# Linear attention with a feed-forward layer on one core: another order of all pieces, half of W1 centred by its column means, and five 4-byte copies among the loads

## The chip, the cores and the metric

The kernel runs on one core of a Trainium2 chip. The number that counts is the device time of one execution in microseconds (us). Of a few runs the median is taken. The core has five engines with queues of their own, each working strictly in order: TensorE (PE, matrix products), VectorE (DVE), ScalarE (ACT), GpSimd (POOL) and SyncE (SP, which here issues all transfers).

## The reference, cut to what matters

Inputs are x (4 x 8 x 768 x 32), decays a, and B and C (4 x 8 x 768 x 16). For each batch and head a state of 16 x 32 is carried along the sequence, and the attention result becomes the input of a feed-forward layer whose normalisation is folded into its first weight.

```python
M = (C_i . B_j) * exp(cum_i - cum_j) * (j <= i)      # inside a chunk
y = M @ x + (C @ state) * exp(cum)                   # plus what entered
state = decay * state + sum_j decay_from_j * B_j x_j
xn = (y - mean(y)) / sqrt(var(y) + 1e-6) * g         # y as tokens x 256
out = y + max(xn @ w1, 0) @ w2                       # w1 256 x 1024, w2 1024 x 256, 64-bit floats
```

## The kernel before, in words

The sequence is cut into 6 steps t of 128 positions; a step holds 4 x 128 = 512 tokens. Every step goes through the attention (scores `G`, weighted scores `R`, what entered `Vi`, values `V`, carried state `Z`, `K`, `S`, its block form `sb`), its output is copied out of PSUM (`y`), split into an upper and a lower float32r part (`yh`, `yl`), turned into token order (`T`, `tc`) and its mean and variance taken (`st`, `ag`, `rs`, `rc`). Then come 8 hidden products `h t m` (line 489, six matrix products of 512 columns each; weight chunk c = m // 4), each followed by `hh` (the relu, upper part) and `hl` (lower part, line 500), which frees the PSUM tile. The second product is `o t b` (line 507, 24 matrix products of 256 columns) or, for step 0, `oc` (line 517, a quarter of the hidden rows at a time); `oe` (line 522) adds the residual and `od` (line 525) stores.

The 64-bit weights are turned into float32 on the chip, half a row block of 128 x 512 at a time: `k0` absolute value of the top word (ACT, line 188), `k1` clamp (DVE, line 193), `k2` shift (DVE, 202), `k3` sign (DVE, 207), `kr` the rest from the low word (ACT, 213), `f` their sum (line 218). W1 is scaled by g and has its column mean taken off: `wc c k` (line 230) does both with two products in float32, against a matrix made from the identity and g (`gm`, lines 220 to 225) and against -g/256; `wh` and `wl` (lines 235, 239) split the result. `wc` is run four times, for (c, k) = (0,0), (0,1), (1,0), (1,1).

PSUM has two pools: 5 buffers `ps_att` for the attention and `oc`, 3 buffers `ps_ffn` for `wc`, `h` and `o`. Results `o` wait for their store in 3 SBUF buffers (pool `p3`), hidden parts in 9 each (pool `hp`).

There is no planner at run time: the order of everything is the text `ISSUE`, a list of pieces. Each piece is put on its engine's queue in that order; a suffix `:v`, `:p`, `:a` chooses VectorE, GpSimd or ScalarE instead of the piece's usual engine. `fill i n` is a product of zeros with n columns that only keeps PE busy. `ld` pieces are loads on SP, `ro` and `ld ud` take the decays of steps 2 to 5 out to memory and back.

Of the kernel before the start of the list is needed to follow the order:

```
ld c 0, l2, ini, ld sel, lr 0, e 0, ld b 0, dc 0, x 0, ld id, ones, rcl, ld w1 0 0, ru, e 1, ld w1 0 1, du 0 0, riv, fill 8 512, rd, ld bt 0, lr 1,
cx 0 0, ld x 0, du 0 1, cx 0 1, ld w1 1 1, x 1, so, ld c 1, B:v 0, dc 1, ld x 1, sm, W:v 0, ld w1 1 0, ld b 1, G 0, du 1 1, ld w2 0, mb, gm:p,
...
k3 1 1 1, ld bt 2, wh 1 0 0, ld c 2, f:v 1 1 0, tc 0 1, ld w2 3, yh:a 0 0, st 0 3, f 1 1 1, ld b 4, G 1, wh 1 0 1, ag 0 3, st 0 1, ld b 2, yh:a 0 1,
ld c 4, be:v 1, Z 0 1, W 1, ld ud 2, wc 1 0, yl 0 1, S 0 1, ld x 2, wl:v 1 0 0, ld ud 4, wl:v 1 0 1, yl 0 0, k0 2 0, R 1 1, h 0 0, ld bt 3, k0 2 2,
R 1 3, be 2, wh 1 1 0, R 1 0, kr 2 0, Z 1, R 1 2, sb 1 0, ld bt 4, hh 0 0, wl:v 1 1 0, K:p 1 0, h 0 1, W 2, k1 2 0, S 1 0, k2 2 0, wc 1 1, c2 1,
```

Of the kernel before, what the change touches and what calls it, by code (L numbers as in the profile page):

```python
# [635 lines left out]
```

## Time and profile before

| | us |
|---|---|
| median of 3 runs | 198.72 (198.05 to 199.54) |
| the profiled execution, whole | 199.18 |
| its span, first to last instruction | 197.4 |
| PE busy, share of the span | 96% |
| DVE busy, share of the span | 65% |
| ACT busy, share of the span | 35% |
| POOL busy, share of the span | 18% |

The rows shown further down come from the profiled execution. Times in them are counted from the start of the span; the 1.78 us between the span and the whole lie around it. A row of the timeline names the engine, the line, what is written and read, and in brackets how long the engine was idle before and what ended that. Products in float32 show as two records each. "PE busy" counts the fills as well.

### The profile page before, as it was taken

Reading aid. Unit: us, or ns where it says so; the run is one execution under the profiler, and the core shown is the slowest. Engines: PE = TensorE matmul, PEld = TensorE weight load, DVE = VectorE, ACT = ScalarE, POOL = GpSimd, SP = SyncE. Lnnn points to the kernel's source line nnn. Section 1 sums busy time; section 2 is a strip of 40 time slices with the busy share of each in tenths; the row PEclk is TensorE's granted clock in tenths of the full one; section 3 lists DMA queues with packets and bytes.
Section 4 is the critical chain, followed back from the end, with each engine's and each line's share of the span. In section 5 each row is a group of like instructions: output and inputs, shape, how many; then the busy total and the mean of one; then the engine's idle time right before and its main releaser. Section 6 shows DMA issues by size and latency. Waiting matters only on the chain.

```text
span 197.4 us, 6404 instructions
## 1 busy us (share of the span) xinstructions
PE 188.8 (96%) x2854; PEld 162.5 (82%) x2854; DVE 129.1 (65%) x273; ACT 69.3 (35%) x127; POOL 35.7 (18%) x41
## 2 busy tenths in 40 slices
PE   8997997999999997999999999999999999999992
PEld 8765564877898985998878998789998899988992
DVE  1789998979997847666489913847347581336610
ACT  4648996588263722000152032403002051124000
POOL 0271191654600000310630000405000000000000
PEclk9999999999999999999999999999999999999999
DMA  5999999640050014711000051000021000200002
GB/s 118 286 367 401 375 307 235 202 149 15 3 163 0 0 53 119 220 67 58 3 3 0 3 150 67 3 3 0 11 72 53 0 3 3 80 27 3 19 17 71
DMA packets 11660, 18.42 MB, mean 93 GB/s; under 512 B 2385, under 2 KB 5873, under 8 KB 11633
## 3 DMA queue, kind: packets, MB, share of 16 engines
q1 hardware_dynamic: 11632, 18.02, 28.7%
q8 instruction: 22, 0.36, 0.8%
q14 instruction: 6, 0.04, 0.1%
HBM read 14.74 MB, written 3.28 MB: 91 GB/s over the span
## 4 chain that ended last, share of the span: by engine, by line
PE 90%; DVE 3%; ACT 3%; DMA 2%; issue 1%; POOL 0%; DVEq 0%
PE ph L489 32%; PE po L507 29%; PE pp L517 5%; PE yps L402 4%; PE wc L230 4%; PE G L375 4%; PE idle L534 4%; PE yps L394 3%; PE yt L458 3%; PE Z L414 2%; DMA out_dram<-o 2%; DVE hl L500 1%; DVE o L522 1%; ACT y L441 1%; PE cum L271 1%
## 5 line engine op out<-in xcount | busy, mean ns | idle before, releaser
L507 PE MATMUL po<-w,hh 128*128 128x256 f32 x320 | 56.8, 281 | 0.1
L489 PE MATMUL ph<-yh,w 128*128 128x512 f32 x192 | 53.8, 402 | 0.5 <-DVE hl L500 0.5
L507 PEld LDWEIGHTS po<-w,hh 128*128 128x128 f32 x320 | 49.1, 188 | 1.0 <-DVE hl L500 0.4
L507 PE MATMUL po<-w,hl 128*128 128x256 f32 x160 | 44.7, 279 | 0.0
L494 ACT ACTIVATE hh<-ph 128x512 fp32r<-128x512 f32 x34 | 20.2, 598 | 68.7 <-PE ph L489 59.8
L489 PEld LDWEIGHTS ph<-yh,w 128*128 128x128 f32 x192 | 34.3, 188 | 7.9 <-DVE hl L500 0.8
L500 DVE SCALAR_TENSOR_TENSOR hl<-ph,hh 128x512 fp32r<-128x512 f32 x48 | 32.3, 683 | 11.4 <-ACT hh L494 11.2
L507 PEld LDWEIGHTS po<-w,hl 128*128 128x128 f32 x160 | 30.1, 188 | 0.0
L489 PE MATMUL ph<-yl,w 128*128 128x512 f32 x96 | 29.8, 392 | 0.0
L522 DVE SCALAR_TENSOR_TENSOR o<-po,rstd,ytok 128x256 f32<-128x256 f32 x20 | 9.5, 480 | 27.3 <-PE po L507 27.2
L489 PEld LDWEIGHTS ph<-yl,w 128*128 128x128 f32 x96 | 18.0, 188 | 4.2 <-DVE yl L450 0.3
L381 DVE TENSOR_TENSOR R<-G,WW 128x512 f32<-128x512 f32 x24 | 15.7, 677 | 2.4 <-PE G L375 2.4
L450 POOL TENSOR_TENSOR yl<-y,yh 128x512 fp32r<-128x512 f32 x6 | 8.4, 1403 | 35.2 <-DVE yh L447 22.0
L496 DVE TENSOR_SCALAR hh<-ph 128x512 fp32r<-128x512 f32 x14 | 9.5, 681 | 4.9 <-PE ph L489 4.9
L441 ACT COPY y<-yps 128x256 f32<-128x256 f32 x15 | 5.2, 374 | 18.8 <-PE yps L402 15.1
L517 PE MATMUL pp<-w,hh 128*128 128x256 f32 x64 | 11.4, 281 | 0.0
L470 DVE BATCH_NORM_STATS2 st<-ytok 128x6 f32<-128x256 f32 x24 | 9.9, 416 | 1.4 <-ACT ytok L463 1.4
L517 PEld LDWEIGHTS pp<-w,hh 128*128 128x128 f32 x64 | 9.9, 188 | 0.3
L361 ACT COPY WW<-wt 32x1024 f32<-32x1024 f32 x8 | 8.3, 1040 | 5.1 <-DVE R L381 5.0
L534 PE MATMUL idle<-const-float32-0.0 128*128 128x128 f32 (+3 forms) x34 | 9.2, 425 | 0.8 <-PEq L624 0.8
L402 PE MATMUL yps<-R,xt 64*32 64x64 f32 x768 | 9.2, 226 | 0.0
L345 POOL TENSOR_TENSOR bs<-b,ud 128x512 f32<-128x512 f32 x3 | 3.9, 1293 | 28.6 <-DMA b<-in_bn_dram 28.6
(96 smaller groups left out, 229.7 us busy)
## 6 DMA issues: line engine op xcount, KB each, us to landing
raw<-in_w_dram SPq DMA_DIRECT2D x8, 512.0 KB, 9.0
xt<-in_x_dram SPq DMA_DIRECT2D x6, 512.0 KB, 6.0
out_dram<-o SPq DMA_DIRECT2D x24, 128.0 KB, 1.7
ud<-scr SPq DMA_DIRECT2D x8, 256.0 KB
c<-in_cn_dram SPq DMA_DIRECT2D x6, 256.0 KB, 2.8
b<-in_bn_dram SPq DMA_DIRECT2D x6, 256.0 KB, 7.2
bt<-in_bt_dram SPq DMA_DIRECT2D x6, 256.0 KB, 8.9
cf<-in_sums_dram SPq DMA_DIRECT2D x1, 256.0 KB
```

The source lines that it names most:

```text
L381: nc.vector.tensor_tensor(out=R.rearrange("p b i k -> p b (i k)"), in0=tiles.pop(("G", t, q)).rearrange("p b i k -> p b (i k)"), in1=WW.re ...
L402: nc.tensor.matmul(tiles["y", t, g, f][32 * k:32 * k + 32, b], x[r, b * NH + h], tiles["R", t, h // 2][r, b, h % 2], start=(t + f + b == 0 ...
L450: e.tensor_tensor(out=tiles["yl", t][:, g], in0=tiles["y32", t][:, g], in1=tiles["yh", t][:, g].bitcast(F32), op=ALU.subtract)
L470: nc.vector.bn_stats(out=st, in_=tiles["ytok", t][:, b])
L489: nc.tensor.matmul(ph, W1[m // 4, k][:, s, mc], v[:, k], start=(i == 0), stop=(i == len(cmb) - 1))
L494: e.activation(h, tiles["ph", t, m], AF.Relu)
L496: e.tensor_scalar(out=h, in0=tiles["ph", t, m], scalar1=0.0, scalar2=None, op0=ALU.max)
L500: nc.vector.scalar_tensor_tensor(out=l, in0=tiles.pop(("ph", t, m)), scalar=0.0, in1=tiles["hh", t, m].bitcast(F32), op0=ALU.max, op1=ALU. ...
L507: nc.tensor.matmul(po, tiles[v, t, m][:, cols], W2[m // 2,][:, s, (m % 2) * DM:(m % 2 + 1) * DM], start=(n == 0), stop=(n == len(cmb) - 1))
L517: nc.tensor.matmul(tiles["po", t, b], tiles[v, t, m][:, cols], W2[m // 2,][:, s, (m % 2) * DM:(m % 2 + 1) * DM], start=(c + n + b % 2 == 0 ...
L522: nc.vector.scalar_tensor_tensor(out=o, in0=tiles.pop(("po", t, b)), scalar=tiles["rstd", t][:, b], in1=tiles["ytok", t][:, b], op0=ALU.mu ...
L534: nc.tensor.matmul(ps[:, :n], zero.to_broadcast([P, P]), zero.to_broadcast([P, n]), start=True, stop=True)
```

## The change

Every piece keeps its arithmetic except the centring of chunk 0 of W1 and the engine that some pieces run on. The parts are:

1. For chunk c = 0 of W1, `wc 0 0` and `wc 0 1` (two products each) are replaced by one `wm 0` (two products with -g/256 that give the column mean times g for both row blocks) and two VectorE instructions `wf 0 k`, each of which scales its 128 x 512 block by g and adds the mean out of PSUM. Chunk 1 keeps `wc`, and it is now loaded, converted and used first (`h 0 4` is the first hidden product).
2. `gm` runs on ScalarE and no longer computes +g/256 apart.
3. The whole list is written anew: other positions, other engines for some pieces, and 9 fills instead of 17. To name the larger shifts between engines, VectorE gets four more of `cm`, two more each of `hh`, `y`, `yh`, and the two `wf`, and loses two each of `K`, `c2`, `f`, `wl`; GpSimd gets two more each of `K`, `c2`, `f`, `wl` and loses `gm`, one `W` and three `sb`; ScalarE gets four `sb`.
4. Five pieces `pc` on SP copy 4 bytes of a tile that a load filled into a tile that nobody reads. Each waits until that load has landed, and the loads behind it in the list wait with it.
5. Results get a pool of 6 buffers (before: 3), hidden parts 10 each (before: 9), `R` 9 (before: 8).

```diff
-    rp = pool("rp", 8)
-    hp = pool("hp", 9)
+    rp = pool("rp", 9)
+    hp = pool("hp", 10)
+    op = pool("op", 6)
...
+    def after(i, what, *at):
+        src = W1[at].bitcast(F32) if what == "w1" else W2[at].bitcast(F32) if what == "w2" else tiles[(what, *at)]
+        src = src.rearrange("p r d -> p (r d)") if what == "x" else src
+        nc.sync.dma_start(seen[:, 8 * i:8 * i + 1], src[:1, :1])
...
     def centring(e=nc.vector):
-        e.tensor_scalar(out=gm, in0=gt, scalar1=1.0 / DM, scalar2=None, op0=ALU.mult)
-        e.tensor_scalar(out=gneg, in0=gt, scalar1=-1.0 / DM, scalar2=None, op0=ALU.mult)
-        for k in range(KC):
-            e.tensor_scalar(out=gd[:, k], in0=ident, scalar1=gt[:, k:k + 1], scalar2=gm[:, k:k + 1], op0=ALU.mult, op1=ALU.subtract)
+        if e is nc.scalar:
+            e.activation(gneg, gt, AF.Copy, scale=-1.0 / DM)
+            for k in range(KC):
+                e.activation(gd[:, k], ident, AF.Identity, bias=gneg[:, k:k + 1], scale=gt[:, k:k + 1])
...
+    def mean_of(c):
+        w = centre[c] = ps_ffn.tile([P, 512], F32, tag="ffn", name=f"wm{c}")
+        for k in range(KC):
+            nc.tensor.matmul(w, gneg[:, k:k + 1].to_broadcast([P, P]), f32[1, c, k], start=(k == 0), stop=(k == KC - 1))
+
+    def less_mean(c, k):
+        f = f32[1, c, k]
+        nc.vector.scalar_tensor_tensor(out=f, in0=f, scalar=gt[:, k:k + 1], in1=centre[c], op0=ALU.mult, op1=ALU.add)
...
     def diagonal(t, f, e=nc.gpsimd):
-        e.tensor_tensor(out=sb, in0=tiles[("S", *before(t, f))], in1=blkt.unsqueeze(1).to_broadcast([P, NB, 2 * HD]), op=ALU.mult)
+        S = tiles[("S", *before(t, f))]
+        if e is nc.scalar:
+            for i in range(2):
+                e.activation(sb[:, :, i * HD:(i + 1) * HD], S[:, :, i * HD:(i + 1) * HD], AF.Copy, scale=even[:, i:i + 1])
...
     def finished(t, b):
-        o = tiles["o", t, b] = p3.tile([P, DM], F32, tag="o", name=f"o{t}{b}")
+        o = tiles["o", t, b] = op.tile([P, DM], F32, tag="o", name=f"o{t}{b}")
...
+fill 0 512, ld la, ld sums, ld mask, ld c 0, fill 1 512, ld w1 1 1, l1, ini, l2, lr 0, dc 0, ld id, ones:v, ld b 0, e 1, ld sel, du 0 0, fill 2 128,
+ld w1 1 0, fill 3 64, x 1, fill 4 256, cx 0 1, ld bt 0, so, ld x 0, cx 0 0, k0 1 1 1, fill 5 256, ld as, fill 6 256, sm, lr 1, k1 1 1 1, e 0, W:v 0,
+du 0 1, fill 7 256, kr 1 1 1, dc 1, mb, x 0, az, B:v 0, k0 1 1 0, k2 1 1 1, G 0, C:v 0, kr 1 1 0, be:v 0, du 1 1, fill 8 128, sp, k1 1 1 0, k3 1 1 1,
+em 0, ld bt 1, ld g, ld w1 0 0, ld w1 0 1, ld c 1, ld w2 0, Z 0 0, em 1, c2:p 0, R 0 0, S 0 0, R 0 1, sb:a 0 1, Z 0 1, f 1 1 1, R 0 3, gm:a, Vi 0,
+R 0 2, V 0 0, k0 1 0 0, k2 1 1 0, V 0 1, k3 1 1 0, y 0 0 0, pc 0 w1 0 1, kr 1 0 1, f:v 1 1 0, wc 1 1, ld x 1, y 0 1 1, rcl, k0 1 0 1, ld w2 3, inv,
+k1 1 0 0, pc 7 bt 0, ru, y 0 0 1, kr 1 0 0, k2 1 0 0, ld w2 1, wc 1 0, k1 1 0 1, ld b 1, be:v 1, ld c 2, k3 1 0 0, ro 0, k2 1 0 1, ld b 2, f:v 1 0 0,
+pc 2 w1 0 0, k3 1 0 1, ld bt 2, riv, f:v 1 0 1, rd, ro 1, ld x 2, wh 1 1 1, y 0 1 0, du 1 0, yh:a 0 1, T 0 1, C 1, wh 1 1 0, Z 1, yh:a 0 0, T 0 0,
+yl 0 1, tc 0 1, wm 0, tc 0 0, W 1, wl:v 1 1 0, yl 0 0, wl:v 1 1 1, h 0 4, ld bt 3, wf 0 0, K:p 0 1, st 0 3, B 1, wf 0 1, h 0 5, hh 0 4, S 0 1,
+wh 1 0 1, ld ud 2, K 1 0, wh:v 1 0 0, cm 1 0, h 0 6, S 1 0, cm 1 1, wl:v 1 0 0, sb 1 1, kr 2 3, hl 0 4, G 1, hh 0 6, wl 1 0 1, ag 0 3, st 0 0,
+hh 0 5, hl 0 6, k0 2 1, h 0 2, R 1 0, c2:p 1, kr 2 0, R 1 2, k0 2 0, sb 1 0, h 0 1, R 1 3, hh 0 2, K:p 1 1, R 1 1, C 2, hl 0 2, W 2, Vi 1, hl 0 5,
...
+st 5 1, h 5 6, ag 5 1, hl 5 7, hh 5 3, hl 5 3, h 5 0, ag 5 0, rs 5, hh 5 6, rc 5, hl 5 6, h 5 5, hh 5 0, hl 5 0, hh 5 5, hl 5 5, o 5 0, o 5 2,
+oe 5 0, od 5 0, od 4 2, od 1 0, od 4 3, o 5 1, o 5 3, oe 5 1, oe 5 2, od 5 1, od 0 2, od 3 0, od 5 2, oe 5 3, od 5 3
```

## Rows read from the trace of the kernel before

**Rows 1.** The page: busy time of each engine over the span.

```profile
PE 188.8 (96%) x2854; PEld 162.5 (82%) x2854; DVE 129.1 (65%) x273; ACT 69.3 (35%) x127; POOL 35.7 (18%) x41
```

**Rows 2.** Busy time by 10 us: PE, PEld, DVE, ACT, POOL, PE clock, DMA share, GB/s.

```profile
0.00:10.00 10.00, 8.75 (x81) 7.81 (x85) 4.86 (x12) 5.78 (x11) 1.45 (x8) 1.00 0.71 201
10.00:20.00 10.00, 8.66 (x268) 5.98 (x251) 9.45 (x17) 6.39 (x16) 4.41 (x6) 1.00 1.02 387
20.00:30.00 10.00, 9.75 (x147) 5.63 (x147) 9.77 (x20) 9.86 (x18) 6.12 (x6) 1.00 1.06 337
...
50.00:60.00 10.00, 10.00 (x249) 9.29 (x248) 9.86 (x23) 4.43 (x9) 2.54 (x3) 1.00 0.26 82
...
70.00:80.00 10.00, 8.77 (x168) 6.98 (x168) 6.92 (x17) 1.60 (x3) 0.00 (x0) 1.00 0.39 122
```

**Rows 3.** The chain of waits in order of time: start, duration, what.

```profile
20.82 3.44 PE wc L230 x8
24.26 1.24 PE G L375 x59
...
41.64 0.79 PE Z L414 x53
...
108.15 11.20 PE po L507 x96
...
193.76 0.48 DVE o L522
```

**Rows 4.** Timeline, PE and VectorE: from `be` of step 0 to the first hidden product.

```profile
12.80 1.25 DVE L354 TENSOR_TENSOR be<-bt,pend 128x512 f32<-128x512 f32 x1
...
26.49 1.28 DVE L239 TENSOR_TENSOR w<-wc,w 128x512 fp32r<-128x512 f32 x2
...
27.43 1.49 PE L489 MATMUL ph<-yh,w 128*128 128x512 f32 x4
```

**Rows 5.** Groups by line: count, busy us, mean ns of one, idle before.

```profile
L381 DVE TENSOR_TENSOR R<-G,WW 128x512 f32<-128x512 f32 x24 | 15.7, 677 | 2.4 <-PE G L375 2.4
...
L450 POOL TENSOR_TENSOR yl<-y,yh 128x512 fp32r<-128x512 f32 x6 | 8.4, 1403 | 35.2 <-DVE yh L447 22.0 <-ACT yh L447 13.1
...
L207 DVE SCALAR_TENSOR_TENSOR top<-raw,top 128x512 int32<-128x512 int32 x8 | 5.3, 687 | 0.1
...
L326 POOL TENSOR_TENSOR cs<-c,ud 128x512 f32<-128x512 f32 x3 | 3.8, 1272 | 2.9 <-issue 2.9
...
L202 DVE TENSOR_SCALAR top<-top 128x512 int32<-128x512 int32 x8 | 3.2, 417 | 0.1
...
L313 DVE TENSOR_TENSOR_SCAN uds<-AZs,ini 128x128 f32<-128x128 f32 x1 | 0.4, 424 | 0.1
```

**Rows 6.** Timeline of the 70s: VectorE's wait for a store, and PE behind it.

```profile
75.34 0.48 DVE L522 SCALAR_TENSOR_TENSOR o<-pp,rstd,ytok 128x256 f32<-128x256 f32 x1 [2.79 <-DMA out_dram<-o]
...
75.88 0.84 PE L414 MATMUL Z<-xt,be 64*32 64x64 f32 x62 [0.64 <-DVE o L522]
77.21 1.19 PE L489 MATMUL ph<-yh,w 128*128 128x512 f32 x4 [0.48 <-DVE hl L500]
```

**Rows 7.** Timeline of GpSimd and VectorE at 9 and at 12 us.

```profile
8.94 1.46 DVE L363 TENSOR_TENSOR WW<-wt,cst 128x1024 f32<-128x1024 f32 x1
9.28 1.20 POOL L222 TENSOR_SCALAR gm<-gt 128x2 f32<-128x2 f32 x1
...
10.46 0.21 POOL L223 TENSOR_SCALAR gneg<-gt 128x2 f32<-128x2 f32 x1
...
12.23 1.26 POOL L326 TENSOR_TENSOR cs<-c,ud 128x512 f32<-128x512 f32 x1
```

**Rows 8.** Transfers: KB each and median us from issue to landing.

```profile
raw<-in_w_dram SPq DMA_DIRECT2D x8, 512.0 KB, 9.0
xt<-in_x_dram SPq DMA_DIRECT2D x6, 512.0 KB, 6.0
out_dram<-o SPq DMA_DIRECT2D x24, 128.0 KB, 1.7
```

More of the change, by code (lines that the diff above doesn't have):

```diff
@@ L101, in linear_attention_ffn @@
     gt = cp.tile([P, KC], F32, name="gt")
-    gm = cp.tile([P, KC], F32, name="gm")
     gneg = cp.tile([P, KC], F32, name="gneg")
@@ L230, in centred @@
             nc.tensor.matmul(w, gd[:, k] if j == k else gneg[:, j:j + 1].to_broadcast([P, P]), f32[1, c, j], start=(n == 0), stop=(n == 1))
+    def mean_of(c):
+        w = centre[c] = ps_ffn.tile([P, 512], F32, tag="ffn", name=f"wm{c}")
+        for k in range(KC):
+            nc.tensor.matmul(w, gneg[:, k:k + 1].to_broadcast([P, P]), f32[1, c, k], start=(k == 0), stop=(k == KC - 1))
+    def less_mean(c, k):
+        f = f32[1, c, k]
+        nc.vector.scalar_tensor_tensor(out=f, in0=f, scalar=gt[:, k:k + 1], in1=centre[c], op0=ALU.mult, op1=ALU.add)
     def upper(w, *at, e=nc.scalar):
@@ L234, in upper @@
         t = {1: W1, 2: W2}[w][at] = p1.tile([P, 2, 512], F32R, tag=name, name=name)
-        (e.copy if e is nc.scalar else e.tensor_copy)(t[:, 0], centre[at] if w == 1 else f32[(w, *at)])
+        (e.copy if e is nc.scalar else e.tensor_copy)(t[:, 0], centre.get(at, f32[(w, *at)]) if w == 1 else f32[(w, *at)])
     def lower(w, *at, e=nc.gpsimd):
         t = {1: W1, 2: W2}[w][at]
-        e.tensor_tensor(out=t[:, 1], in0=centre[at] if w == 1 else f32.pop((w, *at)), in1=t[:, 0].bitcast(F32), op=ALU.subtract)
+        e.tensor_tensor(out=t[:, 1], in0=centre.get(at, f32[(w, *at)]) if w == 1 else f32.pop((w, *at)), in1=t[:, 0].bitcast(F32), op=ALU.subtract)
     wt = cp.tile([P, NT, NR], F32, name="wt")
@@ L434, in diagonal @@
         sb = tiles["sbd", t, f] = p2.tile([P, NB, 2 * HD], F32, tag=f"sbd{f}", name=f"sbd{t}{f}")
-        e.tensor_tensor(out=sb, in0=tiles[("S", *before(t, f))], in1=blkt.unsqueeze(1).to_broadcast([P, NB, 2 * HD]), op=ALU.mult)
+        S = tiles[("S", *before(t, f))]
+        if e is nc.scalar:
+            for i in range(2):
+                e.activation(sb[:, :, i * HD:(i + 1) * HD], S[:, :, i * HD:(i + 1) * HD], AF.Copy, scale=even[:, i:i + 1])
+        else:
+            e.tensor_tensor(out=sb, in0=S, in1=blkt.unsqueeze(1).to_broadcast([P, NB, 2 * HD]), op=ALU.mult)
     def gathered(t, g, f, e=nc.scalar):
@@ L543, in linear_attention_ffn @@
     do = dict(
-        ld=load, fill=fill, fillb=fill_small, az=restart, ini=initial, inv=cleared, ones=masks, gm=centring,
+        ld=load, pc=after, fill=fill, fillb=fill_small, az=restart, ini=initial, inv=cleared, ones=masks, gm=centring,
         lr=logs_repeated, dc=since_middle, du=decay_from_middle, rcl=rest_clipped, ru=rest_since, riv=rest_last, rd=rest_till, ro=rest_out, C=scaled_c, cm=parted, cx=parted_at_once, B=scaled_b, c2=inter, be=ended,
@@ L547, in linear_attention_ffn @@
         W=decays, G=score, R=weighted, Vi=entering, V=value, Z=carry, K=kept, S=state_of, sb=diagonal,
-        k0=magnitude, k1=clamped, km=bounded, k2=shifted, k3=signed, kr=rest, f=whole, wc=centred, wh=upper, wl=lower,
+        k0=magnitude, k1=clamped, km=bounded, k2=shifted, k3=signed, kr=rest, f=whole, wc=centred, wm=mean_of, wf=less_mean, wh=upper, wl=lower,
         y=gathered, yh=upper_y, yl=lower_y, T=turned, tc=tokens, st=stats, ag=aggregate, rs=root, rc=inverse,
```

62 lines of the change are left out of this document (27 added, 35 removed).

## The prediction

> **What bounds the kernel now.** I read the page first. PE is busy for 96% of the span, and fills are in that number, so the next view is the busy time by stretches [rows 1, 2]. It shows three regimes. Up to 10 us nothing is full: the loads come in at 201 GB/s. From 10 to 60 us VectorE is the full engine (9.45, 9.77 and 9.86 of 10 in the stretches shown), while PE is filled up with products of zeros and small gaps; the loads run at their fastest here. From 80 us on PE never stops: four second products take 11.20 us end to end, 2.80 each, and the chain of waits is PE alone down to the last `oe` [rows 3]. So there are two ways to win: less work for PE, which counts in full once PE is the bound, and an earlier start of the hidden products, which VectorE and the loads decide. A third is the one hole inside: at 72 us VectorE waits 2.79 us for a store to give back one of three `o` buffers, and behind it PE stands still for 0.64 and 0.48 us [rows 6].
>
> **The change part by part.**
>
> *The centring.* Eight records of `wc` take 3.44 us [rows 3], which is two pieces of two float32 products, so a piece costs 1.72. Four pieces become two `wc` and one `wm`, which also has two products: PE loses 1.72 us. VectorE pays for it with two `wf`. No row shows `wf`; the nearest is a 128 x 512 instruction with one operand in PSUM, `R` at 677 ns [rows 5]. From below it can't be under the 417 ns of a short one [rows 5], from above it is one of 1.46 us [rows 7], the longest of VectorE here. I take 0.65 each, as `R`, 1.3 together. Both lie behind the first hidden product's operands on VectorE's queue and ahead of chunk 0, which the fourth product needs first.
>
> *The start.* Where does the first hidden product begin? In both kernels VectorE's queue is the path from `be 0` on, and `be 0` waits for `bt 0`, ahead of which the old list loads 2106 KB and the new one 2042. So both start it near 12.8 us [rows 4]; there is no gain in the loads of step 0. From there to the pair of `wl` that the first product needs the old kernel takes 26.49 + 1.28 - 12.80 = 14.97 us, and its product begins at 27.43 [rows 4]. In the new list I count 26 VectorE instructions from `be 0` to the second `wl:v 1 1 k`: fifteen long ones (four `R`, four `k3`, three `f`, two `be`, two `wl`) at 0.65 end to end, as two `wl` in 1.28 show [rows 4], 9.75 us; eight short ones (three `k1`, three `k2`, two scans) at 0.42 [rows 5], 3.35; and three small ones that I estimate at 0.15, 0.45. That is 13.55 us, so the pair ends at 26.35, 1.4 earlier. `G 0` comes later than before, since `B:v 0` stands behind `W:v 0` and the first `k1`; but `R` stands behind `be 0` now, so that costs nothing.
>
> That sum holds only if GpSimd leaves VectorE alone. A GpSimd instruction on 128 x 2 took 1.20 us while VectorE's `WW` ran, and its like took 0.21 right after it; `be 0` took 1.25 us because GpSimd's `cs` ran until 13.49 [rows 4, 7]. So two instructions that both read SBUF through these engines go one after the other. In the new list `C 1` (1.27 us) and `yl 0 1` (1.40 us) [rows 5] reach GpSimd when VectorE still has `f`, `k3` and a scan to do. Below they cost nothing, above both in full, 2.7. The nearest row is `be 0`, which lost 1.25 - 0.65 = 0.6 us to a `cs` of 1.26, near half; half of 2.7 would be 1.35, and I take 1.2, because the scan at the end may pass ahead. The first product then starts 1.4 - 1.2 = 0.2 us earlier, at about 27.2.
>
> The Trainium skill says this outright (SBUF — State Buffer, "Who interferes with whom"): VectorE and GpSimd share one pair of ports as an exclusive lock, and the later one blocks for the whole instruction. It agrees with the 1.20 against 0.21 us above [rows 7]; by it the full 2.7 us would be the sum where VectorE has nothing else in its queue.
>
> *What PE still has to do at that point.* Before, three `wc` and `G 1` lie ahead of the first product and one `wc` and `Z 1` behind it. Now two `wc`, `wm` and `Z 1` lie ahead and `G 1` behind. Ahead is nearly the same; behind, 1.72 + 0.95 (53 products of `Z` in 0.79, so 64 in 0.95) becomes 1.14 (64 of `G`, by 59 in 1.24, at most 1.3) [rows 3]: 1.5 us less, and the 1.72 of the centring is inside this number.
>
> *From the first product to 55 us.* PE follows VectorE here, through the three PSUM buffers that `hl` frees. The list gives VectorE 3.3 us more in the whole kernel, summed over the shifts of pieces, and part of it falls here. Walking down the list with the same durations I find PE waiting about as long as before (for `R 1 1`, for `hl 0 0`, for `sb:v 2 1`), so I put 0, with 1.0 for the better and 1.5 for the worse.
>
> *Result buffers.* By the list at most six `o` wait for their stores at once, so the pool of 6 never blocks: the two gaps of 0.64 and 0.48 us go, 1.1 us [rows 6]. What is late next there is `hl 1 0`, in the shadow of a product. From above the gain is this, from below nothing.
>
> *The other parts.* Fewer fills cost nothing as long as the granted clock stays at 1.00, that is 2.4 GHz, as it did through the old gaps [rows 2]; from 12 to 19 us PE has more idle time than before. `gm` goes to ScalarE, which is not full before 20 us. The `pc` pieces cost SP a wait, priced with the rivals. At the end four stores are issued between the last `oe` pieces, but a product of 2.80 us [rows 3] lies between and a store lands in 1.7 [rows 8]: 0.
>
> **Sum**, against the profiled execution: 199.18 - 0.2 - 1.5 - 1.1 = 196.4. The median of the runs is 0.46 below that execution, so on its scale the sum gives 195.9, and that is the forecast.
>
> **The rivals.** *VectorE takes it back.* The lock costs the full 2.7 us at the start and PE's saved time turns into waiting, since until 55 us the `hl` come at VectorE's pace and that has more to do. The start is 2.7 - 1.4 = 1.3 later; 1.5 less work, 1.1 from the buffers, and 0 to 1.0 lost up to 55 us: 197.9 to 198.9 on the profiled scale, 197.4 to 198.4 on the median's. For it speaks VectorE's 9.8 of 10 [rows 2]; against it that ScalarE takes `sb` and GpSimd more of `K`, `c2` and `f`.
>
> *The other side, slower: `x 1` comes too late.* `pc 0` holds SP until `w1 0 1` has landed, and `ld x 1` stands right behind it. Ahead of and with `w1 0 1` are 4155 KB; at 201 GB/s to 10 us and 387 after [rows 2] that is about 16 us, with the landing about 17.5. `x 1` is issued at 18 and needs 4 us if the queue is short, 6.0 as the median `x`, 9.0 as a median weight block [rows 8]: 22, 24 or 27 us. PE's queue has `Z 1` at about 22.5, and behind it `T 0 0`, `wm 0` and the first product. `Z 1`, one `T` and `wm` take 0.95 + 0.4 + 1.72 = 3.1, so a landing up to 24.1 is hidden by VectorE's 27.2, and each microsecond after it moves everything. The 1.5 and the 1.1 that the rest gains are used up when the first product starts 2.6 later than before, at 30.0, so from a landing at 26.9 the kernel is slower. At 27 it is 199.3 on the profiled scale; `pc 2` holds `bt 2` and `x 2` in the same way, and with 1 to 2 us more for them it is 200.3 to 201.3.
>
> *It doesn't do what it says*: the means are multiplied, but `wf` and its PSUM buffer delay chunk 0 so that PE waits as long as it saves. Then 1.7 of the sum goes: 197.6. I count it with the first rival.
>
> **How the numbers follow.** The forecast, with its own range of 194.3 to 196.9, has 0.55. VectorE taking it back, 196.9 to 198.8, has 0.28. The late `x 1`, near 200, has 0.12. A clock that falls in the thinner stretch from 12 to 19 us has 0.05 (at 1.2 GHz the 3.4 us of `wc` would take 6.9). The best bounds together give 199.18 - 1.4 - 1.5 - 1.1 - 1.0 = 194.2, on the median's scale 193.7; the worst that I leave inside is the first rival's 198.4 with the rest of the 1.5 and some of the late load, 199.6. A difference of about 1%, 2 us, is what a measurement of this kernel tells from no change. Below 196.7 lies nearly all of the forecast and a little of the best of the others, 0.56; above 200.7 the late load for the most part, the clock and the lock's worst, 0.14; the rest is 0.30.
>
> **What would show it.** Right: `wm` and `wc` together in 12 records; the first hidden product before 27.4 us; no wait of `oe` for a store; PE without a gap from 60 us on. Wrong: GpSimd's `cs` and `yl` or VectorE's `f` and `k3` near 23 us at twice their usual time; `Z 1` waiting for `xt`; a granted clock below 1.00 before 190 us. The forecast falls if the first product starts after 28.5 us, or if PE shows new gaps of over a microsecond behind 60 us.

## The result, and the profile after

The changed kernel takes 196.81 us (median of 18 runs, 195.77 to 198.06). Against the kernel before, run beside it on the same chip, the ratio is 0.9895 (95% interval 0.986 to 0.9931): faster by 1.05%. Runs of the kernel before reached from 198.05 to 204.89 us there, and the ratio leaves the disturbed ones out. The forecast was 195.9, so the size is off by 0.9 us and lies inside the range. That is luck in good part: the start alone came 2.12 us later than the sum had it, and 1.56 us of gains that the sum did not hold (1.10 and 0.46, below) stood against that.

The profiled execution took 198.06 us, the slowest of the 18. A later profile of the same kernel (called "again" here, the last experiment) took 196.99, near the median, and stands beside it. In nine of the 18 runs the mean granted clock was 0.991, in the other nine, as in these two profiles, 0.979 to 0.983 (medians 196.70 and 196.81 us).

| us | before | changed | again |
|---|---|---|---|
| first hidden product starts | 27.43 | 29.35 | 28.59 |
| first `o` product (`po`) starts | 79.06 | 77.57 | 76.84 |
| last `po` ends | 193.73 | 193.07 | 191.99 |
| span | 197.4 | 196.3 | 195.2 |

The start, forecast 0.2 us earlier, came 1.92 later (1.16 in the other profile). All of the gain, and more, lies between the first hidden product and the first `po`: 51.63 us before, 48.22 after.

The page of the changed kernel, busy time, and from its part on DMA queues the row of the queue that brings the engines their instructions (packets, MB, share):

```profile
PE 187.3 (95%) x2834; PEld 160.3 (82%) x2834; DVE 131.0 (67%) x278; ACT 67.0 (34%) x128; POOL 38.3 (20%) x40
...
q8 instruction: 22, 0.36, 0.7%
```

The changed kernel's busy time by 10 us, and two finer stretches, with the columns of [rows 2]:

```profile
10.00:20.00 10.00, 7.39 (x277) 5.74 (x279) 9.44 (x19) 6.01 (x17) 3.45 (x5) 0.90 0.86 311
20.00:30.00 10.00, 10.00 (x131) 5.34 (x119) 5.56 (x12) 7.70 (x16) 4.06 (x4) 0.76 0.92 310
...
70.00:80.00 10.00, 9.75 (x121) 8.49 (x121) 9.80 (x25) 1.68 (x4) 0.98 (x1) 1.00 0.40 133
...
18.00:22.00 4.00, 3.33 (x123) 2.62 (x124) 1.92 (x7) 2.17 (x6) 0.00 (x0) 0.50 0.76 257
```

Compare them with [rows 2]. The column to look at is the last but two, the granted clock of TensorE: 1.00 throughout before, 0.90 and 0.76 now, and 0.50 (1.2 GHz) from 18 to 22 us. In the same rows VectorE, full before at 9.77 from 20 to 30 us, is busy for only 5.56, and PE is "busy" for 10.00 because up to 24.8 us, where the clock comes back, its products take twice as long. In the 70s the hole is closed: 9.75 against 8.77. The chain of waits says what happened first:

```profile
16.90 1.77 issue
18.67 2.03 PE yps L421 x114
20.70 5.68 PE wc L240 x8
26.82 0.79 PE Z L433 x53
27.61 0.59 PE yt L482 x4
28.20 1.72 PE wm L245 x4
29.92 4.11 PE ph L513 x18
...
91.24 0.56 issue
```

The eight records of `wc` take 5.68 us instead of 3.44 [rows 3]. Ahead of them stands "issue", 1.77 us in which PE waited for nothing that the profile shows: it stands still within `V`, all of whose operands are there. The clock fell inside this gap, at 17.97. From 18.67 to the first hidden product the chain is PE alone. The timeline of PE, VectorE and GpSimd in this stretch:

```profile
18.67 2.03 PE L421 MATMUL yps<-R,xt 64*32 64x64 f32 x121 [1.77 <-issue]
20.63 2.08 PE L240 MATMUL wc<-top,gd 128*128 128x512 f32 x2
...
25.36 1.02 PE L240 MATMUL wc<-top,gneg 128*128 128x512 f32 x2
...
21.70 0.43 DVE L200 TENSOR_SCALAR top<-top 128x512 f32<-128x512 f32 x1 [2.08 <-ACT top L195]
...
24.18 0.68 DVE L214 SCALAR_TENSOR_TENSOR top<-raw,top 128x512 int32<-128x512 int32 x1
...
24.90 0.69 DVE L225 CUSTOM_DVE_ANT_0 top<-top,low 128x1024 uint16<-128x1024 uint16 x1
25.51 0.41 DVE L338 TENSOR_TENSOR_SCAN uds<-AZs,inv 128x128 f32<-128x128 f32 x1
27.04 1.29 DVE L258 TENSOR_TENSOR w<-wc,w 128x512 fp32r<-128x512 f32 x2 [1.11 <-ACT w L254]
...
25.94 1.28 POOL L345 TENSOR_TENSOR cs<-c,ud 128x512 f32<-128x512 f32 x1 [9.60 <-DMA c<-in_cn_dram]
27.18 2.50 POOL L474 TENSOR_TENSOR yl<-y,yh 128x512 fp32r<-128x512 f32 x2
```

Two products of `wc` take 2.08 us at the lower clock and 1.02 once it is back. VectorE now waits for others: 2.08 us for ScalarE's `top`, which stands behind a `y` that waits for `V`, and 1.11 for `wh`, which waits for `wc`. GpSimd's `cs` and `yl`, which the prediction feared, arrive when VectorE's `k3` (0.68), `f` (0.69) and scan (0.41) are over, and none of these is longer than usual.

The last thing to see is the 70s, where [rows 6] had VectorE wait 2.79 us for a store. From the timeline of VectorE and PE:

```profile
74.13 0.48 DVE L546 SCALAR_TENSOR_TENSOR o<-pp,rstd,ytok 128x256 f32<-128x256 f32 x1
...
75.87 1.20 PE L394 MATMUL G<-cm,bs 32*64 32x128 f32 x64 [0.16 <-DVE cm L355]
```

No `o` waits for a store any more, and PE's one gap there that counts is of 0.16 us.

**The account**, from the profiled executions, needs rows of the kernel before: two of its chain of waits at the first hidden product, and one from the timeline of its PE just behind it:

```profile
26.08 1.91 PE wc L230 x4
27.99 1.40 PE ph L489 x6
...
30.85 0.63 PE L414 MATMUL Z<-xt,be 64*32 64x64 f32 x38 [1.10 <-issue]
```

PE stood still there for 1.10 us in the middle of `Z 1`, a gap of the same kind as the 1.77 above. Start +1.92. From the first hidden product to the first `po`, kernel before: 51.63 us, of them 1.12 behind the store [rows 6] and this 1.10, so 49.41 of work; changed: 48.22, of them 0.16 of gaps, 48.06. That is -1.35 of work, -0.96 of waits and -1.10 of "issue". From the first `po` to the last: 114.67 before, without a gap; 115.50 now, with "issue" gaps of 0.56 and 0.46 (at 91.24 and 108.35 us), so +1.02 and -0.19. Behind the last `po`: 3.67 before, 3.21 now, -0.46. Together -1.12, which is the difference of the executions.

### The profile page after: what moved, and what is told of

It reads as the page before. It is cut to its first block, busy times and chain, and to the rows that moved or that the text cites. A ratio compares the mean times of both kernels' runs of the same rounds, so it can differ in the third digit from the quotient of the medians.

```text
span 196.3 us, 6366 instructions
## 1 busy us (share of the span) xinstructions
PE 187.3 (95%) x2834; PEld 160.3 (82%) x2834; DVE 131.0 (67%) x278; ACT 67.0 (34%) x128; POOL 38.3 (20%) x40
## 4 chain that ended last, share of the span: by engine, by line
PE 89%; DMA 3%; DVE 3%; issue 2%; ACT 1%; SPq 1%
PE ph L513 34%; PE po L531 29%; PE pp L541 6%; PE yps L421 5%; PE yps L413 3%; PE yt L482 3%; DMA raw<-in_w_dram 3%; PE G L394 3%; PE wc L240 3%; PE Z L433 2%; DVE o L546 1%; PE wm L245 1%; SPq L164 1%; DVE WW L382 1%; DVE bs L364 0%
## 5 line engine op out<-in xcount | busy, mean ns | idle before, releaser
L518 ACT ACTIVATE hh<-ph 128x512 fp32r<-128x512 f32 x32 | 18.8, 598 | 57.7 <-PE ph L513 41.2
L474 POOL TENSOR_TENSOR yl<-y,yh 128x512 fp32r<-128x512 f32 x5 | 7.1, 1423 | 63.9 <-ACT yh L471 62.0
L520 DVE TENSOR_SCALAR hh<-ph 128x512 fp32r<-128x512 f32 x16 | 10.9, 684 | 7.1 <-PE ph L513 7.0
L421 PE MATMUL yps<-R,xt 64*32 64x64 f32 x768 | 9.8, 239 | 1.8 <-issue 1.8
L421 PEld LDWEIGHTS yps<-R,xt 64*32 64x32 f32 x768 | 8.6, 111 | 2.6 <-issue 2.3
L465 ACT COPY y<-yps 128x256 f32<-128x256 f32 x13 | 4.6, 374 | 16.5 <-PE yps L421 10.1
L541 PE MATMUL pp<-w,hl 128*128 128x256 f32 x32 | 8.9, 279 | 0.0
L441 POOL TENSOR_TENSOR K<-S,emt 128x256 f32<-128x256 f32 x6 | 3.8, 639 | 24.2 <-DVE S L449 24.2
```

The lines of the kernel that those rows point to most:

```text
L421: nc.tensor.matmul(tiles["y", t, g, f][32 * k:32 * k + 32, b], x[r, b * NH + h], tiles["R", t, h // 2][r, b, h % 2], start=(t + f + b == 0 ...
L474: e.tensor_tensor(out=tiles["yl", t][:, g], in0=tiles["y32", t][:, g], in1=tiles["yh", t][:, g].bitcast(F32), op=ALU.subtract)
L518: e.activation(h, tiles["ph", t, m], AF.Relu)
L520: e.tensor_scalar(out=h, in0=tiles["ph", t, m], scalar1=0.0, scalar2=None, op0=ALU.max)
L541: nc.tensor.matmul(tiles["po", t, b], tiles[v, t, m][:, cols], W2[m // 2,][:, s, (m % 2) * DM:(m % 2 + 1) * DM], start=(c + n + b % 2 == 0 ...
```

## The experiments

The theory at first: PE ran out of instructions at 16.9 us, the granted clock fell because of it, and the two made the start late. The runs bear out the two, but not that the one needs the other. Rivals: the lock between VectorE and GpSimd, VectorE's own work, or the loads. "First product" is the first hidden product, "first po" and "last po" as in the table. Each ratio is against the kernel before on the same chip.

**Run 1. Fills in the thin stretch.**

```diff
-Z 0 0, em 1,
+Z 0 0, fill 9 256, em 1,
...
-Z 0 1, f 1 1 1, R 0 3, gm:a, Vi 0, R 0 2, V 0 0,
+Z 0 1, fill 10 64, f 1 1 1, R 0 3, gm:a, Vi 0, R 0 2, fill 11 256, V 0 0,
...
-k2 1 1 0, V 0 1,
+k2 1 1 0, fill 12 64, V 0 1,
```

> The changed kernel with four more fills (256, 64, 256 and 64 columns) between Z 0 0 and V 0 1, where PE was thin. Theory: what cost the start is the granted clock, which fell at 18 us behind PE's 1.77 us without an instruction; with PE busier there it stays at 2.4 GHz, the eight records of wc take 3.4 us and not 5.7, the first hidden product starts near 27.0 and not at 29.35, and the ratio to before goes from 0.99 to 0.98 or lower (about 2 us). Rival: VectorE and the loads set the start anyway; the clock stays up, but the first product still starts after 28.8 and the ratio stays within 0.985 to 0.993.

Measured: 204.13 us (200.47 to 206.94; the profiled execution is the 206.94), ratio 1.0118 (0.9995 to 1.0241). First product at 34.56. The timeline of PE shows why, and a second gap of the kind much later:

```profile
18.56 0.84 PE L421 MATMUL yps<-R,xt 64*32 64x64 f32 x63 [1.42 <-issue]
...
25.04 0.31 PE L421 MATMUL yps<-R,xt 64*32 64x64 f32 x1 [4.41 <-issue]
...
114.99 0.27 PE L421 MATMUL yps<-R,xt 64*32 64x64 f32 x2 [1.76 <-issue]
```

PE stood still for 4.41 us one record before the end of `V 0 1`. Of the transfers on the instruction queue (22 of 16 KB each), one runs from 22.68 to 23.63, just ahead of 25.04, and one ends at 17.34, ahead of 18.56. A gap of this kind is called a fetch gap here. Counted in PE's records from the first, the gap at 18.56 stands behind record 221, as it does in the changed kernel; the four fills put other records at that place and did not take the gap away. The clock fell at 20.33, between the two.

**Run 2. Only the place moved**: 52 small products (104 records) at 9 us, where PE has time.

```diff
-fill 6 256, sm,
+fill 6 256, fillb 9 52, sm,
```

> The changed kernel with 52 products of zeros on 32 x 16 in the gap of PE at 8.3 us. They do no work in the stretch from 14 to 18 us; they only put some 200 more instructions ahead of it, so that the place in PE's stream where it ran dry at 16.90 us comes earlier, where PE waits anyway. Theory: the 1.77 us without an instruction belong to that place in the stream and set off the fall of the clock; then the gap before V 0 0 goes, the clock stays up, and the kernel gains 2 to 3 us on the changed one. Rival: the clock falls because the stretch is thin; then the gap goes but the granted clock still drops to 1.2 GHz between 15 and 25 us and at most 1 us is gained.

Measured: 196.61 us (196.5 to 196.92), ratio 0.9893 (0.9829 to 0.9957). The clock was at 0.50 from 17.07 to 23.9 all the same, first product 29.17. The timeline of PE:

```profile
16.19 0.98 PE L433 MATMUL Z<-xt,be 64*32 64x64 f32 x64 [1.89 <-DVE R L400]
18.09 1.13 PE L413 MATMUL yps<-c,sbd 32*64 32x64 f32 x32 [0.92 <-issue]
```

The labels mislead here. `Vi` reads `sbd`, which ScalarE finished at 17.99; in the changed kernel it starts 0.10 us behind `sbd` too, so the 0.92 is a wait for ScalarE. The 1.89 is put down to VectorE's `R`, but that ended at 15.77, 0.42 before `Z 0` goes on, where PE in the changed kernel starts within 0.14 us of what the profile names as its releaser; and there the same products start ahead of the first `R`. A transfer of instructions ends at 14.66, 1.53 before, and the gap stands behind record 222, against 221. So it is the fetch gap, as long as before: the place moved from `V` to `Z 0` by just the records put ahead, and the experiment did not do away with it. The two late gaps of the changed kernel are gone, and the last `po` ends at 191.51. So the place of a gap follows the count of instructions ahead of it.

**Run 3. The kernel before, thinned**: without its fills 9 to 16.

```diff
-ld w2 1, fill 9 256, R 0 2, ro 1, fill 10 128, ld bt 1, fill 11 128, R 0 0, fill 12 512, ld w2 2,
+ld w2 1, R 0 2, ro 1, ld bt 1, R 0 0, ld w2 2,
...
-fill 14 512, du 1 0, be:v 0, em 0, R 0 1, Z 0 0, k1 1 0 1, fill 15 256, S 0 0,
+du 1 0, be:v 0, em 0, R 0 1, Z 0 0, k1 1 0 1, S 0 0,
...
```

> The kernel before without its fills 9 to 16 (10 to 18 us). Theory: fewer fills lower the clock; it drops to 1.2 GHz at some time between 13 and 26 us, wc takes more than 3.44 us per eight records, and the kernel gets 1 to 3 us slower. Rival: the gaps of before are short enough without the fills; clock 1.00 up to 190 us and a time within 0.5 us of before.

Measured: 200.61 us (197.86 to 203.67), ratio 1.0018 (0.996 to 1.0076). Its busy time by 10 us, with the columns of [rows 2]:

```profile
10.00:20.00 10.00, 4.78 (x238) 4.07 (x225) 8.38 (x17) 4.63 (x12) 4.15 (x6) 0.78 0.99 377
20.00:30.00 10.00, 9.41 (x148) 5.60 (x131) 6.50 (x15) 7.89 (x16) 2.37 (x2) 0.71 1.04 347
```

With PE busy for 4.78 of 10 us (8.66 before [rows 2]) the clock falls to 0.78 and 0.71 in the mean, in the old order as well. It fell at 15.54 behind a wait of 4.03 us for `R`, and this execution has no fetch gap of 0.1 us or more. So the fills that the change left out had held the clock, and their absence is enough to let it fall. The first product came 3.64 us later (31.07), yet the first `po` only 0.89 later (79.95): the old order had 2.75 us of slack, of which its three gaps (1.10, 0.64, 0.48) are 2.22. The new order has none there: over the first, second, fourth and sixth runs here and the changed kernel, the first `po` comes 48.12 to 48.23 us behind the first product, which lies anywhere from 27.61 to 34.56. The time in all, though, is no different from that of the kernel before: the 1 to 3 us that had been expected did not come.

**Run 4. Without the 4-byte copies.**

```diff
-y 0 0 0, pc 0 w1 0 1, kr 1 0 1,
+y 0 0 0, kr 1 0 1,
...
-k1 1 0 0, pc 7 bt 0, ru,
+k1 1 0 0, ru,
...
-f:v 1 0 0, pc 2 w1 0 0, k3 1 0 1,
+f:v 1 0 0, k3 1 0 1,
...
```

> The changed kernel without the five 4-byte copies. Theory: they cost nothing and bring nothing, since x 1 lands before Z 1 needs it: ratio as the changed kernel's, 0.985 to 0.993. Rival 1: they hold x 1 and w2 back too long; without them 0.5 to 1.5 us faster. Rival 2: they protect w1 0 0 and w1 0 1; without them k0 of chunk 0 starts over 1 us later and the kernel gets slower by up to 1 us.

Measured: 197.29 us (195.97 to 198.67), ratio 0.9931 (0.9888 to 0.9974). Clock at 0.50 from 16.02 to 22.85, fetch gap of 1.30 us that begins only at 16.57, first product 27.98, last `po` 191.93. The interval overlaps that of the changed kernel: the copies cost and bring nothing that this measures.

**Run 5. Fills, and two loads later**: the fills of the first run, with `ld w2 3` and `ld w2 1` moved behind `ro 1`, so that fewer bytes are in flight when PE fetches.

```diff
-k0 1 0 1, ld w2 3, inv,
+k0 1 0 1, inv,
...
-k2 1 0 0, ld w2 1, wc 1 0,
+k2 1 0 0, wc 1 0,
...
-rd, ro 1, ld x 2,
+rd, ro 1, ld w2 3, ld w2 1, ld x 2,
```

> The changed kernel with the four fills of the first experiment and with ld w2 3 and ld w2 1 moved behind ro 1, so that 1 MB less is on the rings between 18 and 26 us. Theory: PE runs dry in V 0 0 and V 0 1 because the transfer that brings its next instructions waits behind loads; with these two moved, the gap of 4.4 us of the first experiment shrinks to under 1.5, the clock stays up or falls for less than 4 us, the first hidden product starts at 26.5 to 28.0, and the second products start 48.2 us after it; 2 to 3 us faster than the changed kernel. Rival: the gap has to do with the instructions, not with the loads; it stays at 4 us, and the first product starts after 32.

Measured: 203.42 us (201.84 to 204.2), ratio 1.0203 (1.0114 to 1.0292). The clock stays at 1.00 until 30.81 us, through fetch gaps of 0.67 and 1.48 us, and `wc` takes 3.63, yet the first product begins at 30.27. VectorE and GpSimd:

```profile
24.68 1.78 DVE L214 SCALAR_TENSOR_TENSOR top<-raw,top 128x512 int32<-128x512 int32 x1
...
26.49 1.64 DVE L225 CUSTOM_DVE_ANT_0 top<-top,low 128x1024 uint16<-128x1024 uint16 x1
28.05 1.49 DVE L338 TENSOR_TENSOR_SCAN uds<-AZs,inv 128x128 f32<-128x128 f32 x1
29.46 1.26 DVE L258 TENSOR_TENSOR w<-wc,w 128x512 fp32r<-128x512 f32 x2
...
24.63 1.28 POOL L345 TENSOR_TENSOR cs<-c,ud 128x512 f32<-128x512 f32 x1 [8.92 <-DMA b<-in_bn_dram]
25.86 3.40 POOL L474 TENSOR_TENSOR yl<-y,yh 128x512 fp32r<-128x512 f32 x2
```

Here is the lock that the prediction had in its sum. `k3` takes 1.78 instead of 0.68, `f` 1.64 instead of 0.69, the scan 1.49 instead of 0.41: 3.13 us, each beside one GpSimd instruction. The late `V` and `wc` of the changed kernel had hidden it by making GpSimd's operands late. Its ratio is 3.1% above the changed kernel's. What the lock does not explain lies behind the first product: the clock falls to 0.50 from 30.81 to 34.22, and the first `po` comes 50.28 us behind the first product instead of 48.22; then gaps of 0.83 (ending at 94.08) and 1.76 us (in `V` of step 4, ending at 112.22), a clock of 0.59 in the mean from 112 to 116 us, and 118.65 us from the first `po` to the last instead of 115.50.

**Run 6. The two loads later, alone**, with the fills as in the changed kernel.

```diff
-k0 1 0 1, ld w2 3, inv,
+k0 1 0 1, inv,
...
-rd, ro 1, ld x 2,
+rd, ro 1, ld w2 3, ld w2 1, ld x 2,
```

> The changed kernel with ld w2 3 and ld w2 1 moved behind ro 1 alone. Theory: the instructions come sooner, the gap before V 0 0 stays near 1.3 to 1.8 (what is ahead of it on the rings, w1 0 0 and w1 0 1, is not moved), the clock still falls in the thin stretch, so the first product starts at 28 to 29.4 and the time is 0 to 1.3 us under the changed kernel's. Rival: w2 comes too late; the first oc or k0 of step w2 waits, and the kernel is 1 us or more slower.

Measured: 198.48 us (196.69 to 199.58), ratio 0.9961 (0.9911 to 1.0012). The second instruction transfer now ran at 19.02 us instead of 22.80, but the first gap stayed (1.06 us) and the clock fell (0.50 from 15.29 to 22.12); first product 27.61. PE:

```profile
17.89 2.00 PE L421 MATMUL yps<-R,xt 64*32 64x64 f32 x121 [1.06 <-issue]
```

The gap begins at 16.82, 1.53 us after the clock fell; in the fourth run it begins 0.55 and in the seventh 1.26 us after. From 9 us to the fall PE's longest wait in this run was 0.43. So here the fall can't come from the fetch gap: the thin stretch ahead of it is enough, as in the third run. The scan met `cs` and took 1.50. The loads are not the lever by themselves.

**Run 7. `wc` for both chunks.**

```diff
-tc 0 1, wm 0, tc 0 0,
+tc 0 1, wc 0 0, wc 0 1, tc 0 0,
...
-ld bt 3, wf 0 0, K:p 0 1, st 0 3, B 1, wf 0 1, h 0 5,
+ld bt 3, K:p 0 1, st 0 3, B 1, h 0 5,
...
-sb 1 1, kr 2 3,
+sb 1 1, wl:v 1 0 1, kr 2 3,
...
-hh 0 6, wl 1 0 1, ag 0 3,
+hh 0 6, ag 0 3,
```

> The changed kernel with wc 0 0 and wc 0 1 in place of wm 0 and the two wf, and the lower part of block (0, 1) on VectorE. Theory: PE is the bound from the first product on, so the 1.72 us of the two products that come back count in full: first product 1.7 later and the second products 1.2 to 1.9 later, ratio to before near 1.00. Rival: VectorE paces PE up to 55 us and gets 1.5 us back from the two wf less one lower part; the second products start within 0.7 us of the changed kernel's.

Measured: 201.06 us (200.81 to 202.04), ratio 1.0108 (1.002 to 1.0196), against 0.9895 with `wm`. First `po` at 79.34, 1.77 later than in the changed kernel, where the prediction put 1.72 on the centring. That the two agree is in part luck. The first product came only 0.82 later (30.17), since the clock was back 4.46 us after the fetch gap here and 6.13 in the changed kernel; and most of the other 0.95 is a wait for VectorE's `wl`:

```profile
32.91 1.19 PE L513 MATMUL ph<-yh,w 128*128 128x512 f32 x4 [0.79 <-DVE w L258]
```

The last `po` is 2.46 later, with 0.70 more of "issue" gaps behind the first one. The two `wf`, 0.75 and 0.73 us each, cost nothing that could be seen: dropping them, for one `wl` more on VectorE, did not help.

**Run 8. The kernel before with six result buffers.**

```diff
+    op = pool("op", 6)
...
-        o = tiles["o", t, b] = p3.tile([P, DM], F32, tag="o", name=f"o{t}{b}")
+        o = tiles["o", t, b] = op.tile([P, DM], F32, tag="o", name=f"o{t}{b}")
```

> The kernel before with 6 buffers for results in place of 3, nothing else. Theory: the wait of 2.79 us for a store and PE's gaps of 0.64 and 0.48 us behind it go: 0.8 to 1.2 us faster, ratio 0.994 to 0.996. Rival: VectorE or PE finds another wait there at once (VectorE is behind with hl 1 0 anyway): within 0.4 us of before, and PE's stretch from 70 to 80 us is as thin.

Measured: 199.51 us (196.63 to 204.97), ratio 0.9938 (0.9878 to 0.9997). The 70s of this run:

```profile
72.14 0.48 DVE L523 SCALAR_TENSOR_TENSOR o<-pp,rstd,ytok 128x256 f32<-128x256 f32 x1 [1.15 <-PE pp L518]
```

No `o` waits for a store and PE is busy for all of 70 to 80 us. 0.6% of 199 is 1.2 us, against 1.1 in the prediction; the interval reaches from 0.1 to 2.4. The profiled execution, 199.25 us, is no faster than that of the kernel before (199.18), since its first product came 0.77 later (28.20) and fetch gaps of 0.31 and 1.76 us stand where the other has one of 1.10:

```profile
37.89 1.35 PE L403 MATMUL yps<-R,xt 64*32 64x64 f32 x112 [1.76 <-issue]
```

PE's list of products is the same in the two, so the size of these gaps is no fixed price of a kernel.

**Run 9. As many PE instructions as in the changed kernel**, to part the fills' effect at the start from that of the shifted places behind it; the two loads come later as in the fifth run.

```diff
-fill 2 128, ld w1 1 0, fill 3 64, x 1, fill 4 256,
+fill 2 448, ld w1 1 0, x 1,
...
-fill 5 256, ld as, fill 6 256,
+fill 5 512, ld as,
...
-Z 0 0, em 1,
+Z 0 0, fill 9 256, em 1,
...
-Z 0 1, f 1 1 1, R 0 3, gm:a, Vi 0, R 0 2, V 0 0,
+Z 0 1, fill 10 64, f 1 1 1, R 0 3, gm:a, Vi 0, R 0 2, fill 11 256, V 0 0,
...
```

> Edit: the changed kernel with three more fills in the thin stretch (256 columns behind Z 0 0, 64 behind Z 0 1, 256 before V 0 0), with ld w2 3 and ld w2 1 behind ro 1, and with the first fills merged (2, 3 and 4 into one of 448 columns, 5 and 6 into one of 512), so that TensorE has the same number of instructions as in the changed kernel. Theory A (what cost the fuller kernel 3 us behind the second products was that its extra instructions moved a fetch of TensorE's instructions into a bad place; what it cost at the start was the lock): clock at 1.00 through wc, wc 3.44, the first hidden product still near 30, since cs and yl lie beside k3, f and the scan as before (k3, f, scan together over 4 us instead of 1.8), po 48.2 to 50.3 behind it, but from the first po to the last 115 to 116 instead of 118.65; median about 200 to 201, ratio 1.00 to 1.01. Rival B (fills by themselves cost late time): first po to last 118 or more again, ratio 1.02.

Measured: 198.83 us (196.88 to 200.59), ratio 1.0002 (0.995 to 1.0054). Late, theory A held: 115.50 us from the first `po` to the last, no gap in `V` of step 4; the fetch gap behind record 2004 is 0.61 us and lies in a hidden product again, as the 0.46 of the changed kernel does. At the start it missed in the profiled execution: PE stood still for 1.62 us up to 18.59, the clock was at 0.66 and 0.50 in the mean from 18 to 22, and only the scan met GpSimd (1.50 us); first product 27.93. That execution is the fastest of the ten. Seven of the ten kept a mean clock of 1.00 (197.58 to 200.59 us), three, this one among them, did not (0.991; 196.88 to 199.19). That would fit a lock that comes out where the clock holds, but the two groups overlap and none of the seven is in a profile, so it is not shown.

**Run 10. The same, without GpSimd beside VectorE.**

```diff
-T 0 1, C 1, wh 1 1 0,
+T 0 1, wh 1 1 0,
...
-yl 0 1, tc 0 1, wm 0, tc 0 0, W 1, wl:v 1 1 0, yl 0 0, wl:v 1 1 1, h 0 4, ld bt 3, wf 0 0,
+tc 0 1, wm 0, tc 0 0, W 1, wl:v 1 1 0, wl:v 1 1 1, yl:v 0 0, yl:v 0 1, h 0 4, ld bt 3, wf 0 0, C:v 1,
```

> Edit: as the run before, and C 1, yl 0 0 and yl 0 1 run on VectorE behind the pair of wl (C 1 behind wf 0 0), so that GpSimd has nothing beside VectorE's k3, f and scan. Theory A (clock and lock are what separates the start of 29.35 from the forecast's 27.2, and each of them alone brings out the other): clock at 1.00 through wc, wc 3.44, k3 0.68, f 0.69, scan 0.41, first hidden product 27.3 to 28.3, second products 48.2 to 49.5 behind it (VectorE has 2 us more to do there), first po to last 115 to 116; ratio 0.975 to 0.985, below the changed kernel of the same call. Rival B (VectorE's own work, not the lock, holds the product): first product at 29 or later with all VectorE durations nominal, ratio 0.99 or above.

Measured: 196.78 us (196.58 to 199.0), ratio 0.9884 (0.9779 to 0.999); clock at 1.00 in all of its runs. PE, VectorE and GpSimd:

```profile
17.51 1.56 PE L421 MATMUL yps<-R,xt 64*32 64x64 f32 x121 [0.84 <-issue]
18.99 1.12 PE L240 MATMUL wc<-top,gd 128*128 128x512 f32 x2
...
25.66 1.49 PE L513 MATMUL ph<-yh,w 128*128 128x512 f32 x4
...
31.07 1.20 PE L394 MATMUL G<-cm,bs 32*64 32x128 f32 x64 [0.28 <-issue]
...
37.28 1.34 PE L421 MATMUL yps<-R,xt 64*32 64x64 f32 x111 [0.63 <-issue]
...
11.65 0.68 DVE L373 TENSOR_TENSOR be<-bt,pend 128x512 f32<-128x512 f32 x1
...
22.63 0.69 DVE L214 SCALAR_TENSOR_TENSOR top<-raw,top 128x512 int32<-128x512 int32 x1
...
23.35 0.69 DVE L225 CUSTOM_DVE_ANT_0 top<-top,low 128x1024 uint16<-128x1024 uint16 x1
23.96 0.42 DVE L338 TENSOR_TENSOR_SCAN uds<-AZs,inv 128x128 f32<-128x128 f32 x1
24.29 1.26 DVE L258 TENSOR_TENSOR w<-wc,w 128x512 fp32r<-128x512 f32 x2
...
24.41 1.27 POOL L364 TENSOR_TENSOR bs<-b,ud 128x512 f32<-128x512 f32 x1 [8.35 <-DMA b<-in_bn_dram]
```

The two causes taken away together, the first product begins at 25.66: 3.69 earlier than in the changed kernel's profile, 2.93 earlier than in its other one. Of these 3.69, 0.23 is there at the start of `V`, 1.41 more by the start of `wc` (0.93 of the gap, the rest `V` at the higher clock), 2.05 more at the end of `wc`. So the start is settled: dry PE and fallen clock made it late, side by side, and the lock stood ready behind them.

The end is not what theory A hoped for (48.2 to 49.5 us from the first product to the first `po` and a ratio up to 0.985; it was 50.09 and 0.9884). Against the other profile of the changed kernel the 2.93 are 1.09 at the first `po` and 0.72 at the last. The tenth run's busy time by 10 us:

```profile
20.00:30.00 10.00, 9.84 (x99) 6.17 (x98) 9.82 (x20) 8.37 (x16) 1.27 (x1) 1.00 0.89 276
30.00:40.00 10.00, 9.09 (x278) 7.07 (x277) 9.97 (x22) 8.09 (x15) 5.68 (x6) 1.00 0.52 173
```

VectorE is full again from 20 to 40 us (9.82 and 9.97 of 10), and the three pieces it took over cost it 2.04 us. From the first product to the first `po` there are 1.87 us more than in the changed kernel: 0.63 is a fetch gap (behind record 601), 0.16 and 0.28 are waits for VectorE's `wf` and for ScalarE's `cm` behind it (`cm` is done at 30.97, `G 1` starts at 31.07), and the rest shows no gap. Later fetch gaps of 0.60 and 0.45 us stand behind records 1622 and 2004, as in the changed kernel. So an early start was given back, a third of it to a fetch gap; that the rest went at VectorE's pace fits the full engine, but is not shown.

**Run 11. The changed kernel again**, as the measure for the last two.

> Edit: none, the changed kernel once more, on the chip of the two runs before. Both theories: ratio 0.986 to 0.993 as before; the clock at 0.50 from about 18 to 24 us and wc above 5 us; first hidden product 28 to 29.5; first po 48.2 behind it.

Measured: 197.04 us (196.84 to 197.73), ratio 0.9878 (0.9813 to 0.9943), clock 0.979 to 0.983 in the mean in all four runs, first `po` 48.25 behind the first product. The version of the run before, 196.78, beats the kernel before but can't be told from this one.

## Why the prediction was right or wrong

*The start: wrong, by the most.* The step that failed is "Fewer fills cost nothing as long as the granted clock stays at 1.00, that is 2.4 GHz, as it did through the old gaps", with the chance of 0.05 for "A clock that falls in the thinner stretch". The clock fell to 0.50 at 17.97 us, and the first product came 1.92 us later than before, not 0.2 earlier. The old gaps were short because the old fills stood in them; the thinned kernel before shows that without them the clock falls there too, and in three runs of the new order it fell before PE ran dry. The price had been foreseen in kind (3.4 us of `wc` to 6.9; it took 5.68), not the likelihood, though the prediction itself said that PE would have more idle time from 12 to 19 us. Not foreseen at all was that PE can lack instructions. The kernel before shows it, 1.10 us of "issue" in `Z 1` at 29.75 us, and the prediction counted that stretch as work. Nor was "VectorE's queue is the path" right for either profile: the chain of waits goes through PE there, from 19.84 us on in the kernel before (`wc` in [rows 3], then the rows above) and from 18.67 in the changed one.

*VectorE's 13.55 us: right where it applied.* Without lock and at full clock the forecast's own numbers put the first product at 27.43 - 1.4 = 26.0; the tenth run, whose chain goes through VectorE there, measured 25.66. From `be 0` to the end of the pair it took 13.90 us (11.65 to 25.55), 1.04 of them a wait for ScalarE; that `be 0` began 1.15 earlier than the 12.8 of the forecast made up for it.

*The lock: right in kind, wrong in size, and hidden.* Taken at 1.2 with an upper bound of 2.7, it cost nothing in the changed kernel and 3.13 where the clock held. The bound of 2.7 counted two GpSimd instructions, `C 1` and `yl 0 1`; the third, `yl 0 0`, met VectorE as well, and three met instructions lost 1.10, 0.95 and 1.08. The Trainium skill (SBUF — State Buffer, "Who interferes with whom") says which meet: a VectorE instruction with two inputs in SBUF contends with a GpSimd one that reads SBUF, and one with at most one input there, outside the two-port modes, does not. The trace agrees: `k3` with two took 1.78, while the pair of `wl`, with one of its inputs in PSUM, took its usual 1.26 beside `bs`.

*Less work, -1.5: right.* -1.35 up to the first `po`; the centring alone 1.77 there by the seventh run, against 1.72, an agreement that is in part luck, as said there.

*Nothing from the first product to 55 us: right in work, but* the fetch gap of 1.10 went, by the luck of the place. *Result buffers, -1.1: right* (-0.96 in the account; 0.6% in the eighth run, with a wide interval).

*Behind 60 us no gap: wrong.* Two fetch gaps, 1.02 us together, and what lies behind the last `po` is 0.46 shorter, which the prediction put at 0. What brought that 0.46 was not tried, and the late gaps differ between the two profiles of the same kernel (0.56 and 0.46, then 0.12 and 0.65).

*The rivals.* The late `x 1` did not come: `Z 1` waited for nothing, and the kernel without the copies is no different. "VectorE takes it back" was not the cause in the changed kernel, and whether it is what limits the tenth run stays open. For the profiled execution the sum gave 196.4 and 198.06 was measured, 1.66 more: 2.12 at the start, 0.15 in the work, 0.14 at the buffers and 0.83 behind the first `po`, less 1.10 for the gap in `Z 1` and 0.46 at the end (the sum of these is 1.68). The median lies nearer, 0.9 above the forecast, since that execution was the slowest. The prediction said that it falls if the first product starts after 28.5 us; it started at 29.35, and at 28.59 in the other profile, so the forecast falls by its own condition.

## What to carry to other kernels

Read the granted clock and the "issue" gaps of TensorE before pricing a stretch by the other engines: fills that look like waste may hold the clock, and taking them out can use up the work saved (here the start came 1.92 us later, for 1.35 of work). A start that comes earlier is worth only as much as the rest of the order lets through (2.93 us became 0.72 here), and two engines that wait for each other's ports may be kept apart by a delay that you are about to remove. Count instructions as well as work: with four more products (eight records) ahead of it a gap of 0.46 us at 108 us became one of 1.76 at 112 to 115. And look at what a waiting instruction reads before you believe the label of its gap.
